# Halving the planner's slack between score pairs, and rearranging its two ends, in a fused attention and feed-forward kernel

## The chip, the cores and the metric

One core of a Trainium2 chip. The metric is the device time of one execution in microseconds (us). PE is TensorE, PEld its weight loads, DVE is VectorE, ACT is ScalarE, POOL is GpSimd, SP is SyncE; SPq and ACTq are the instruction queues that issue transfers. The time of a kernel is the median of its fast runs; ratios are the mean time of one kernel's fast runs over that of the other's fast runs of the same rounds, so they are not quite the ratio of the medians quoted. A profile covers one execution, and its span is some 1.7 us shorter than that run's time.

## The reference, cut to what matters

```python
x = A_x                                      # 2048 x 512, bf16
g = sigmoid((x * gate_w).sum(-1))            # one gate per row
qkv = x @ wqkv                               # 32 heads of width 16
p = softmax(q @ k.T / 4)                     # 2048 x 2048 for each head
a = (p @ v) @ wo
b = (silu(x @ w_gate) * (x @ w_up)) @ w_down # hidden width 1792
return g * a + (1 - g) * b
```

The exponentials of 32 x 2048 x 2048 scores are the bulk of the elementwise work.

## The kernel before

The program is written out by a planner in Python. A *unit* is the attention of four heads for 512 queries; there are 32, each of 64 *blocks* of 128 keys by 512 queries of one head. Two blocks form a *score pair*: TensorE writes it to one of two PSUM tiles `s_t`, ScalarE takes its exponential to `e_t`. Some blocks go to VectorE instead (`d_t`, then `y_t`), four to a *group*, with a chain of six further instructions. In what remains of the gap between two score pairs, TensorE does value products (`e_t` or `y_t` times `vaug`) and pieces of two matmuls of the projections and the feed-forward. The planner keeps an estimated clock for each engine, and lets a piece in if it overshoots the moment at which the next score tile comes free by at most `SLACK`:

```python
    def side(most):                          # the next projection or feed-forward piece, if it fits
        ...
        if t is None or t > plan.pe + 0.1 or 0.226 * mms + (0.1 if plan.mode != "F" else 0.0) > most:
            return None
        return c
...
    SLACK = 0.2
...
        room = s_end[pairs[0] % 2] - plan.pe
        if room > 0.02:
            if to_vector() and not d_wait and d_end[0] <= plan.pe + 0.05:
                vset.add(nxt)
                emit_d(nxt)                  # a block for VectorE has first call
                ...
            n_pv = pvs_ready(plan.pe)
            switch = 0.0 if plan.mode == "C" else 0.1
            fits = int((room + SLACK - switch) / 0.216)
            ...
            c = side(room + SLACK)
            if n_pv and fits > 0 and (...):
                emit_pv()                    # value products of one step
                ...
            if c is not None:
                pace.credit -= emit_piece(c)
                ...
        emit_pair(list(range(nxt, min(nxt + 2, nb))))
```

The start, up to the first score pair. The largest |k| of each head times |q| bounds the scores, and is subtracted ahead of the exponential:

```python
    act(out=q0r[:, :], in_=qp0[:, :], func=ACT.Copy)
    for i in range(2):
        vec.tensor_reduce(out=kpart0[:, i:i + 1], in_=kp0[i][:, :], axis=AX.X, op=ALU.max,
                          apply_absolute_value=True)
        vec.tensor_copy(out=ones_h[i][:], in_=onescol[:])
        act(out=kaug[:, 0, ...], in_=kp0[i][:, :], func=ACT.Identity, bias=ones_h[i][:, 0:1], scale=1.0)
        if i == 0:
            vec.tensor_scalar(out=aq0[:, :].bitcast(U16), in0=q0r[:, :].bitcast(U16), scalar1=0x7FFF,
                              scalar2=None, op0=ALU.bitwise_and)
        v0(8 * i)                            # values of the first heads: 32 small matmuls
    vec.tensor_scalar(out=kneg1, in0=bsel0, scalar1=kpart0[:, 0:1], ...)
    vec.scalar_tensor_tensor(out=kneg0, in0=bsel0, scalar=kpart0[:, 1:2], in1=kneg1, ...)
    mm(bp0[:, :], lhsT=kneg0, rhs=aq0[:, :], start=True, stop=True)
```

The end, after the last value product: `last_mm` works through the four row tiles in the order 2, 0, 1, 3.

```python
    for tq in range(TQ):
        vec.tensor_tensor(out=on_l[:, cs], in0=osb[:, cs], in1=rps[:, cs], op=ALU.mult)
    last_mm(1, on_l)
    act(out=scaled[:, :], in_=a_ps[2][:, 0:D], func=ACT.Identity, scale=gval[:, t:t + 1])
    nc.gpsimd.tensor_tensor(out=mt[:, 2, :], in0=scaled[:, :], in1=acc[0][:, 2, :], op=ALU.add)
    for tq in (0, 1, 3):
        store(qb * TQ + tq, a_ps[tq], acc[0][:, tq, :], mt[:, tq, :])    # VectorE, then a store from SyncE
    nc.sync.dma_start(out=out_f[t * P:(t + 1) * P, :], in_=mt[:, 2, :])
```

Of the kernel before, what the change touches and what calls it, by code (L numbers as in the profile page):

```python
# [8 lines left out]
ACT = mybir.ActivationFunctionType  # L9
ALU = mybir.AluOpType  # L10
# [3 lines left out]
U16 = mybir.dt.uint16  # L14
# [64 lines left out]
def kernel(  # L79
# [12 lines left out]
    nc = tc.nc  # L92
    P = 128
# [12 lines left out]
    TQ = QBW // P  # L106
    assert H * DH == D and D % P == 0 and F % P == 0 and S % QBW == 0 and G == 8 and TQ == 4
    out_f = out.flatten_outer_dims()
# [37 lines left out]
    def ordered(ins):  # L146
        i = ins.ins
        if i.engine in last_of:
            tc.add_manual_dep(
                i, last_of[i.engine].name,  # L150
                mybir.DependencyInfo(mybir.DependencyClass.NoSync, mybir.DependencyReason.DATA),
                reason="order",
            )
        last_of[i.engine] = i
        return ins
# [4 lines left out]
    def act(*args, **kw):  # L160
        ordered(nc.scalar.activation(*args, **kw))  # L161
# [7 lines left out]
    vec = Ordered()  # L169
# [6 lines left out]
    for c0 in (0, D):  # L176

        nc.scalar.dma_start(out=wqk[:, :, c0:c0 + 64],
                            in_=A_wqkv[:, c0:c0 + 64].rearrange("(dc p) c -> p dc c", p=P))
# [6 lines left out]
    for c0 in (D, 0):  # L186
        nc.sync.dma_start(out=wqk[:, :, c0 + 64:c0 + D],
                          in_=A_wqkv[:, c0 + 64:c0 + D].rearrange("(dc p) c -> p dc c", p=P))
# [18 lines left out]
    mt = big.tile([P, FC, QBW], BF16, name="mt")  # L207
# [3 lines left out]
    onescol = const.tile([P, 1], F32, name="onescol")  # L211
# [8 lines left out]
    bsel0 = mt[:, 3, 0:P]  # L220
# [3 lines left out]
    for i in range(2):  # L224
        nc.vector.tensor_copy(
            out=wpad[i][:, :, :].rearrange("p dc (j c) -> p dc j c", c=32)[:, :, :, 1:1 + DH],
            in_=wqk[:, :, i * D:i * D + 64].rearrange("p dc (j c) -> p dc j c", c=DH))
# [81 lines left out]
    def m_tile(name):  # L309
        while m_ready() is None:  # L310
            pay()
        plan.pe = max(plan.pe, m_ready())
        m_tiles[0] += 1
        return ps_m.tile([P, QBW], F32, tag="m", name=name)
# [63 lines left out]
    def v0(t0):  # L378

        p = m_tile("vp")  # L380
        for i in range(8):
            for dc in range(DC):
                mm(p[:, 64 * i:64 * i + 64], lhsT=xT[:, dc, (t0 + i) * P:(t0 + i + 1) * P], rhs=wv[:, dc, 0:64],
                   start=(dc == 0), stop=(dc == DC - 1))
        act(out=vaug[:, t0:t0 + 8, 0:4 * VC].rearrange("p t (h c) -> p t h c", c=VC)[:, :, :, 1:1 + DH],
            in_=p[:, :].rearrange("p (t h c) -> p t h c", h=4, c=DH), func=ACT.Copy)
        m_free(0.0)
# [433 lines left out]
    def store(t, a_ps, base, o_t=None):  # L821
        if o_t is None:
            o_t = opool.tile([P, D], BF16, tag="ot", name="o_t")[:, :]
        vec.scalar_tensor_tensor(out=o_t, in0=a_ps[:, 0:D], scalar=gval[:, t:t + 1], in1=base,
                                 op0=ALU.mult, op1=ALU.add)
        nc.sync.dma_start(out=out_f[t * P:(t + 1) * P, :], in_=o_t)
# [35 lines left out]
    qp0 = m_tile("qp0")  # L862
# [7 lines left out]
    kpart0 = const.tile([P, 2], F32, name="kpart0")  # L870
    ones_h = [const.tile([P, 1], F32, name=f"ones_h{i}") for i in range(2)]
    aq0 = work.tile([P, QBW], BF16, tag="aq", name="aq0", bufs=4)
    q0r = work.tile([P, QBW], BF16, tag="qst", name="q0r")
    kneg0 = mt[:, 3, P:2 * P]
    kneg1 = mt[:, 3, 2 * P:3 * P]
    act(out=q0r[:, :], in_=qp0[:, :], func=ACT.Copy)
    for i in range(2):
        vec.tensor_reduce(out=kpart0[:, i:i + 1], in_=kp0[i][:, :], axis=AX.X, op=ALU.max,
                          apply_absolute_value=True)
        vec.tensor_copy(out=ones_h[i][:], in_=onescol[:])  # L880
        act(out=kaug[:, 0, i * 2 * QBW:(i + 1) * 2 * QBW], in_=kp0[i][:, :], func=ACT.Identity,
            bias=ones_h[i][:, 0:1], scale=1.0)
        if i == 0:
            vec.tensor_scalar(out=aq0[:, :].bitcast(U16), in0=q0r[:, :].bitcast(U16), scalar1=0x7FFF, scalar2=None,
                              op0=ALU.bitwise_and)
        v0(8 * i)
    vec.tensor_scalar(out=kneg1, in0=bsel0, scalar1=kpart0[:, 0:1], scalar2=None, op0=ALU.mult)
    vec.scalar_tensor_tensor(out=kneg0, in0=bsel0, scalar=kpart0[:, 1:2], in1=kneg1,
                             op0=ALU.mult, op1=ALU.min)
    bp0 = ps_d.tile([P, QBW], F32, tag="d", name="bp0")  # L890
    mm(bp0[:, :], lhsT=kneg0, rhs=aq0[:, :], start=True, stop=True)
    for v in range(2):
# [1 line left out]
    for v in range(2):  # L894
        vec.scalar_tensor_tensor(out=q0[0][:, v, :], in0=bp0[:, :], scalar=vsel[:, v:v + 1],
                                 in1=q0[0][:, v, :], op0=ALU.mult, op1=ALU.add)
# [3 lines left out]
                            op0=ALU.is_gt, op1=ALU.mult)  # L900
    vec.scalar_tensor_tensor(out=bsel[:, :], in0=lo_t[:], scalar=0.5, in1=far_t[:],
                                   op0=ALU.is_lt, op1=ALU.mult)
# [50 lines left out]
    for qb in range(QB):  # L953
        a0 = f0 + per * qb
        for fc in range(FC):
            load, pcs = gu[(qb, fc)]
            i = order_.index((qb, fc))
# [117 lines left out]
    def side(most):  # L1075

        due = any(not c.out() for n in range(plan.slot, plan.slot + 12) for c in need.get(n, []))
        c = pace.next(plan.slot) if pace.credit > 0 or due else None
        if c is None:
            return None  # L1080
        mms, _, takes = c.pieces[c.i]
        t = m_ready() if takes else 0.0
# [3 lines that stand above are left out]
# [3 lines left out]
            pay_v() if vops else pay_d() if d_wait else pay()  # L1089
        emit_pv()  # L1090

    SLACK = 0.2
    def to_vector():

        un, at_ = divmod(nxt, 4 * KT)
        if vcur:
            if nxt % 4 in [b % 4 for b in vcur["b"]]:
                return 0
            return 2 if at_ >= 4 * KT - 4 * (NV - vcur["i"]) else 1
        if nxt < 16 or at_ > (50 if un < UNITS - 1 else 12) or y_live[0] >= 3 or sum(v[0] for v in vops) > 6:  # L1100
            return 0
        return 1

    while nxt < nb:
# [12 lines left out]
        if room > 0.02:  # L1117
# [6 lines left out]
            switch = 0.0 if plan.mode == "C" else 0.1  # L1124
            fits = int((room + SLACK - switch) / 0.216)
            crowded = pairs[0] - min(e_left.values(), default=pairs[0]) >= EB - 4
            c = side(room + SLACK)
            if n_pv and fits > 0 and (plan.mode == "C" or n_pv > 1 and fits > 1 and (pv_turn[0] or c is None)
# [59 lines left out]
               lhsT=rt[:, 4 * tq + j:4 * tq + j + 1].broadcast_to([P, 32]), rhs=ident[:, :],  # L1188
               start=True, stop=True, tile_position=(0, 32 * j), skip_group_check=True)
    on_l = work.tile([P, QBW], BF16, tag="rd", name="on_l")  # L1190
    for tq in range(TQ):
        cs = slice(tq * P, (tq + 1) * P)
        vec.tensor_tensor(out=on_l[:, cs], in0=osb[:, cs], in1=rps[:, cs], op=ALU.mult)
    last_mm(1, on_l)

    t = qb * TQ + 2
# [2 lines left out]
    nc.gpsimd.tensor_tensor(out=mt[:, 2, :], in0=scaled[:, :], in1=acc[0][:, 2, :], op=ALU.add)  # L1199
    for tq in (0, 1, 3):  # L1200
        store(qb * TQ + tq, a_ps[tq], acc[0][:, tq, :], mt[:, tq, :])
    nc.sync.dma_start(out=out_f[t * P:(t + 1) * P, :], in_=mt[:, 2, :])



# [28 lines left out]
```

## Time and profile before

| | before |
|---|---|
| time | 872.04 us (871.99 to 873.24) |
| span of the profile | 869.8 us |
| start, to the first exponential | 18.26 us |
| middle, first to last exponential | 840.74 us, 880 exponentials |
| end, from the start of the last exponential | 10.80 us |

The three parts sum to the span, and the edits fall into them one by one. These rows of the table by stretches have start and end, length, busy time and number of instructions of each engine, then the mean granted clock as a share of full speed, and DMA:

```profile
838.00:843.00 5.00, 3.43 (x32) 0.95 (x33) 4.90 (x11) 5.00 (x6) 0.00 (x0) 1.00 0.00 0
843.00:847.00 4.00, 4.00 (x22) 0.68 (x15) 2.24 (x5) 3.33 (x4) 0.00 (x0) 0.57 0.00 0
847.00:859.00 12.00, 9.70 (x69) 2.78 (x68) 6.33 (x8) 11.86 (x13) 0.00 (x0) 1.00 0.00 1
```

In the second row the clock is 0.57: 3.4 us of the 4 ran at half speed. ScalarE, busy all the time before, is busy 3.33 of 4.00 there.

### The profile page before, as it was taken

How to read it: one execution, taken by the hardware profiler on the slowest of the kernel's cores; microseconds unless marked ns; L12 is line 12 of the kernel's file. 1: busy time of each engine (PE TensorE's matmuls, PEld its weight loads, DVE VectorE, ACT ScalarE, POOL GpSimd, SP SyncE). 2: the span in 40 equal slices, each digit the busy share in tenths (PEclk: the TensorE clock that was granted, in tenths of full speed). 3: DMA queues.
4: the chain of work that ended last, by engine and by line, in shares of the span. 5: the costliest groups of instructions: out<-in, count | busy, mean ns of one | idle time of the engine just before them, and what ended most of it. 6: DMA issues, size and time to landing. Idle time of an engine off the chain costs nothing.

```text
span 869.8 us, 14419 instructions
## 1 busy us (share of the span) xinstructions
PE 798.7 (92%) x5232; PEld 208.8 (24%) x5232; DVE 796.5 (92%) x1117; ACT 842.7 (97%) x944; POOL 8.6 (1%) x31
## 2 busy tenths in 40 slices
PE   5999999999999999999999989989998989889985
PEld 2222222222222222222222222222222222222221
DVE  7889999999999999999999999989999999998974
ACT  3999999999999999999999999999999999999995
POOL 3000000000000000000000000000000000000000
PEclk9999999999999999999999999999999999999999
DMA  8400011111210012211000122110001121100000
GB/s 200 122 1 10 11 38 43 37 41 35 60 31 8 10 42 66 56 50 41 4 6 18 41 49 61 50 35 13 7 17 41 36 61 36 28 10 4 5 20 25
DMA packets 88064, 31.99 MB, mean 37 GB/s; under 512 B 75648, under 2 KB 87544, under 8 KB 87992
## 3 DMA queue, kind: packets, MB, share of 16 engines
q1 hardware_dynamic: 86408, 30.87, 14.5%
q8 instruction: 41, 0.67, 0.3%
q10 hardware_dynamic: 1584, 0.20, 0.1%
q14 instruction: 31, 0.25, 0.1%
HBM read 20.83 MB, written 2.34 MB: 27 GB/s over the span
## 4 chain that ended last, share of the span: by engine, by line
PE 46%; ACT 35%; DVE 8%; issue 8%; SPq 1%; DMA 1%; DVEq 0%; ACTq 0%
ACT e_t L161 33%; PE s_t L158 17%; PE o_ps L158 9%; PE dps L158 5%; PE d_t L158 4%; DVE y_t L167 4%; PE gp L158 3%; ACT th L161 3%; PE up L158 2%; DVE u_t L167 2%; PE a_ps L158 1%; PE qp L158 1%; PE vp L158 1%; PE kp L158 1%; PE x_ps L158 1%
## 5 line engine op out<-in xcount | busy, mean ns | idle before, releaser
L161 ACT ACTIVATE e_t<-s_t 128x1024 bf16<-128x1024 f32 x880 | 819.6, 1090 | 5.4 <-PE s_t L158 4.8
L158 PE MATMUL s_t<-qx,kaug 64*128 64x512 bf16 x1648 | 326.7, 384 | 47.7 <-ACT e_t L161 44.6
L167 DVE TENSOR_SCALAR y_t<-d_t 128x512 uint16<-128x512 f32 x288 | 197.8, 687 | 28.3 <-PE d_t L158 24.5
L158 PEld LDWEIGHTS <-kaug 64*128 64x128 bf16 x2048 | 99.6, 93 | 377.4 <-issue 374.3
L158 PE MATMUL o_ps<-e_t,vaug 128*32 128x512 bf16 x1760 | 172.0, 387 | 0.7 <-ACT e_t L161 0.7
L158 PE MATMUL d_t<-qx,kaug 64*128 64x512 bf16 x272 | 102.5, 377 | 0.6 <-DVE y_t L167 0.6
L167 DVE TENSOR_TENSOR y_t<-y_t,u_t 128x2048 uint16<-128x2048 uint16 x72 | 87.8, 1219 | 1.0
L167 DVE TENSOR_TENSOR u_t<-u_t 128x2048 f16<-128x2048 f16 x72 | 87.6, 1217 | 0.7
L167 DVE TENSOR_TENSOR u_t<-u_t,z_t 128x2048 f16<-128x2048 f16 x72 | 87.6, 1217 | 0.4
L158 PEld LDWEIGHTS <-vaug 128*32 128x32 bf16 x2048 | 45.1, 94 | 133.1 <-issue 130.2
L158 PE MATMUL dps<-wd_t,mt 128*128 128x512 bf16 x224 | 67.8, 384 | 0.0
L158 PE MATMUL gp<-xT,wg 128*128 128x512 bf16 x224 | 67.8, 384 | 0.0
L158 PE MATMUL up<-xT,wu 128*128 128x512 bf16 x224 | 64.7, 383 | 0.0
L167 DVE TENSOR_SCALAR y_t<-y_t 128x2048 uint16<-128x2048 uint16 x72 | 49.5, 688 | 1.2
L167 DVE TENSOR_SCALAR u_t<-z_t 128x2048 f16<-128x2048 uint16 x72 | 49.5, 687 | 0.8
L167 DVE TENSOR_SCALAR z_t<-y_t 128x2048 uint16<-128x2048 uint16 x72 | 49.3, 684 | 0.2
L167 DVE SCALAR_TENSOR_TENSOR mt<-gs,up 128x512 bf16<-128x512 bf16 x56 | 38.2, 682 | 4.7 <-PE up L158 3.4
L167 DVE SCALAR_TENSOR_TENSOR gs<-th,gp 128x512 bf16<-128x512 bf16 x56 | 38.2, 682 | 2.6 <-ACT th L161 2.3
L161 ACT ACTIVATE th<-gp 128x512 bf16<-128x512 f32 x56 | 36.7, 655 | 0.0
L158 PEld LDWEIGHTS <-mt 128*128 128x128 bf16 x263 | 16.2, 99 | 43.2 <-issue 35.1
L158 PE MATMUL s_t<-on,kaug 64*128 64x512 bf16 x112 | 22.4, 383 | 1.8 <-ACT e_t L161 1.4
L158 PEld LDWEIGHTS <-wu 128*128 128x128 bf16 x224 | 14.2, 97 | 30.1 <-issue 24.7
(104 smaller groups left out, 358.0 us busy)
## 6 DMA issues: line engine op xcount, KB each, us to landing
wg<-in_B_w_gate_dram SPq DMA_DIRECT2D x56, 128.0 KB
wu<-in_B_w_up_dram SPq DMA_DIRECT2D x56, 128.0 KB
on<-osb SPq DMA_DIRECT2D x120, 16.0 KB
rb<-rr SPq DMA_DIRECT2D x15, 128.0 KB
wd_t<-in_B_w_down_dram SPq DMA_DIRECT2D x1, 1792.0 KB
qx<-qst SPq DMA_DIRECT2D x112, 16.0 KB
out_dram<-o_t SPq DMA_DIRECT2D x12, 128.0 KB
kaug<-on SPq DMA_DIRECT2D x20, 64.0 KB
```

The costliest lines, as they stand in the source:

```text
L158: ordered(nc.tensor.matmul(*args, **kw))
L161: ordered(nc.scalar.activation(*args, **kw))
L167: return lambda *a, **kw: ordered(f(*a, **kw))
```

## The change

Its intent: less overshoot in each gap, so that ScalarE finds its scores ready; 0.29 us and one product less on VectorE's chain at the start; and stores that don't queue behind one another at the end. The diff, cut to its core:

```diff
     act(out=q0r[:, :], in_=qp0[:, :], func=ACT.Copy)
+    act(out=aq0[:, :], in_=qp0[:, :], func=ACT.Abs)
     for i in range(2):
         vec.tensor_reduce(out=kpart0[:, i:i + 1], ...)
-        vec.tensor_copy(out=ones_h[i][:], in_=onescol[:])
+        if i == 0:
+            vec.tensor_copy(out=ones_h[0][:], in_=onescol[:])
+            vec.tensor_scalar(out=kneg1, in0=bsel0, scalar1=kpart0[:, 0:1], ...)
+        else:
+            vec.scalar_tensor_tensor(out=kneg0, in0=bsel0, scalar=kpart0[:, 1:2], in1=kneg1, ...)
+            vec.tensor_copy(out=ones_h[1][:], in_=onescol[:])
         act(out=kaug[:, 0, ...], ...)
-        if i == 0:
-            vec.tensor_scalar(out=aq0..., scalar1=0x7FFF, op0=ALU.bitwise_and)
         v0(8 * i)
-    vec.tensor_scalar(out=kneg1, ...)
-    vec.scalar_tensor_tensor(out=kneg0, ...)
...
-    SLACK = 0.2
+    SLACK = 0.1
...
-    for tq in range(TQ):
+    for tq in (2, 0, 1, 3):
         vec.tensor_tensor(out=on_l[:, cs], ...)
...
-    nc.sync.dma_start(out=out_f[t * P:(t + 1) * P, :], in_=mt[:, 2, :])
+    nc.scalar.dma_start(out=out_f[t * P:(t + 1) * P, :], in_=mt[:, 2, :])
```

More of the change, by code (lines that the diff above doesn't have):

```diff
@@ L879 @@
                           apply_absolute_value=True)
-        vec.tensor_copy(out=ones_h[i][:], in_=onescol[:])
+        if i == 0:
+            vec.tensor_copy(out=ones_h[0][:], in_=onescol[:])
+            vec.tensor_scalar(out=kneg1, in0=bsel0, scalar1=kpart0[:, 0:1], scalar2=None, op0=ALU.mult)
+        else:
+            vec.scalar_tensor_tensor(out=kneg0, in0=bsel0, scalar=kpart0[:, 1:2], in1=kneg1,
+                                     op0=ALU.mult, op1=ALU.min)
+            vec.tensor_copy(out=ones_h[1][:], in_=onescol[:])
         act(out=kaug[:, 0, i * 2 * QBW:(i + 1) * 2 * QBW], in_=kp0[i][:, :], func=ACT.Identity,
             bias=ones_h[i][:, 0:1], scale=1.0)
-        if i == 0:
-            vec.tensor_scalar(out=aq0[:, :].bitcast(U16), in0=q0r[:, :].bitcast(U16), scalar1=0x7FFF, scalar2=None,
-                              op0=ALU.bitwise_and)
         v0(8 * i)
-    vec.tensor_scalar(out=kneg1, in0=bsel0, scalar1=kpart0[:, 0:1], scalar2=None, op0=ALU.mult)
-    vec.scalar_tensor_tensor(out=kneg0, in0=bsel0, scalar=kpart0[:, 1:2], in1=kneg1,
-                             op0=ALU.mult, op1=ALU.min)
     bp0 = ps_d.tile([P, QBW], F32, tag="d", name="bp0")
```

## The prediction

> **What bounds the kernel now.** I read the page's busy shares first, then its groups, then the waits of ScalarE, then ScalarE's timeline, and last the timelines of the two ends, where three of the four edits lie.
>
> ```profile
> PE 798.7 (92%) x5232; PEld 208.8 (24%) x5232; DVE 796.5 (92%) x1117; ACT 842.7 (97%) x944; POOL 8.6 (1%) x31
> ...
> L161 ACT ACTIVATE e_t<-s_t 128x1024 bf16<-128x1024 f32 x880 | 819.6, 1090 | 5.4 <-PE s_t L158 4.8
> L158 PE MATMUL s_t<-qx,kaug 64*128 64x512 bf16 x1648 | 326.7, 384 | 47.7 <-ACT e_t L161 44.6
> L167 DVE TENSOR_SCALAR y_t<-d_t 128x512 uint16<-128x512 f32 x288 | 197.8, 687 | 28.3 <-PE d_t L158 24.5
> ```
>
> ScalarE is busy 97%, nearly all of it in 880 exponentials of score pairs; TensorE waits 44.6 us for it. So ScalarE carries the middle. But 5.4 us of idle time understates what can be won: the mean record is 1090 ns, longer than the distance from one exponential to the next, because records overlap. The floor is in the start times:
>
> ```profile
> 399.67 6.58 ACT L161 ACTIVATE e_t<-s_t 128x1024 bf16<-128x1024 f32 x7
> 405.99 0.75 ACT L161 ACTIVATE th<-gp 128x512 bf16<-128x512 f32 x1
> 406.47 5.78 ACT L161 ACTIVATE e_t<-s_t 128x1024 bf16<-128x1024 f32 x6
> 412.68 8.36 ACT L161 ACTIVATE e_t<-s_t 128x1024 bf16<-128x1024 f32 x9 [0.44 <-PE s_t L158]
> ```
>
> Seven exponentials from 399.67 to the tanh at 405.99 are (405.99 - 399.67) / 7 = 0.903 us each; the tanh takes 406.47 - 405.99 = 0.48. The first exponential starts at 18.26, the last at 859.00, as ScalarE's timeline and the chain show: 840.7 us. The floor is 879 x 0.903 + 56 x 0.48 = 820.6. So **20 us in the middle are bubbles**, most too small to be listed as idle. That is all that better spacing can give while the exponentials stay 880.
>
> What makes a bubble, in the timeline of all engines near 202:
>
> ```profile
> 201.67 0.39 PE L158 MATMUL s_t<-qx,kaug 64*128 64x512 bf16 x2
> ...
> 202.00 0.60 PE L158 MATMUL kp<-xT,wqk 128*128 128x512 bf16 x2
> ...
> 202.53 0.40 PE L158 MATMUL o_ps<-e_t,vaug 128*32 128x512 bf16 x3
> ...
> 202.86 0.39 PE L158 MATMUL s_t<-qx,kaug 64*128 64x512 bf16 x2
> ```
>
> Between two score pairs TensorE ran a projection piece and a value product; the next pair then started 1.19 us after the one before, where the floor is 0.90. In the chain of waits the exponentials of this place start at 202.23 and 203.35, 1.12 apart: a bubble of 0.21.
>
> **What the Trainium skill says.** "ScalarE: Activation LUTs", section "Table sets: the hidden batching unit", says that abs is in every table set as filler, so the new Abs should need no further table load. The trace shows the cost of one (1.28 us, once, at 2.37 us) and, agreeing, that Copy, Identity, Exp and Tanh share it. The section "What ACT_TABLE_LOAD costs" says back-to-back activations overlap by about 93 ns; here 1085 (median) - 903 = 182 ns, and I use the trace. "DMA: Bandwidth & Descriptors", section "Issuing engines are not separate DMA queues", says that several issuing engines only save the issue time of the sequencer. The tail below shows that this issue time, and an in-order wait, are what the last stores pay.
>
> **Part 1, queries' magnitudes and first bound.** The start now:
>
> ```profile
> 14.51 0.29 DVE L167 TENSOR_SCALAR aq<-q0r 128x512 uint16<-128x512 uint16 x1
> ...
> 14.72 1.22 DVE L167 TENSOR_REDUCE kpart<-kp 128x1 f32<-128x1024 f32 x1
> ...
> 16.19 0.35 DVE L167 SCALAR_TENSOR_TENSOR mt<-mt,kpart 128x128 bf16<-128x128 bf16 x1
> 16.46 0.61 DVE L167 TENSOR_SCALAR qx<-q0r,vsel 128x512 bf16<-128x512 bf16 x2
> ...
> 17.03 1.41 DVE L167 SCALAR_TENSOR_TENSOR qx<-bp,vsel,qx 128x512 bf16<-128x512 f32 x2
> ```
>
> VectorE is the chain here. The mask of 0.29 us leaves it and the first product of the bound (0.24) takes that place, so the second maximum starts at about the same 14.7. After it, instead of copy, product, combination (15.93 to 16.55 in the chain), only the combination remains: some 0.35 us earlier. Against this, ScalarE gets an Abs of a 512-wide tile out of PSUM, start to start about 0.48 like the tanh. It pushes the two copies of keys back by about 0.3, and since the projection's PSUM tile is freed only after it, the second block of first-head values waits to about 15.0 instead of 14.7. TensorE had 0.89 us idle before the bound's matmul, so this is hidden. I put **-0.35 us** on the first exponential (18.26 to about 17.9).
>
> **Part 2, the tail.**
>
> ```profile
> 862.39 0.88 DVE L167 TENSOR_TENSOR on_l<-osb,rps 128x128 bf16<-128x128 bf16 x4 [0.52 <-PE rps L158]
> 863.13 0.54 PEld L158 LDWEIGHTS <-on_l 128*128 128x128 bf16 x4 [0.97 <-DVE on_l L167]
> ...
> 864.33 1.26 POOL L1199 TENSOR_TENSOR mt<-scaled,kaug 128x512 bf16<-128x512 f32 x1 [856.03 <-ACT scaled L161]
> 865.32 0.74 DVE L167 SCALAR_TENSOR_TENSOR mt<-a_l,gval,kaug 128x512 bf16<-128x512 f32 x1
> 865.62 0.36 SPq L1202 DMA_DIRECT2D out_dram<-mt  x1
> 866.08 1.37 SPq L826 DMA_DIRECT2D out_dram<-mt  x3
> ```
>
> TensorE takes tile 2 first, but VectorE makes it third. Making it first takes two steps of 0.22 off: -0.44 on the path over ScalarE, GpSimd and VectorE. The larger thing is the queue: the store of tile 2 stands first in it and waits for GpSimd (864.33 + 1.26 = 865.59), and the other three follow at 0.46 each, the last at about 867.0, though two of their tiles were ready by 865.4. On ScalarE's queue tile 2 goes at about 865.2 by itself, and the last of the three is issued when its data are ready: 866.06 - 0.44 + 0.1 = 865.7. So the last issue moves by 867.0 - 865.7 = **-1.3 us**, the first part included. The transfers fill the engines for about 0.5 us each, so they don't collide.
>
> **Part 3, the slack, and where I chose.** The program plans each gap and lets a piece of TensorE work in when it ends at most SLACK after the next score tile comes free. I went through the planner's decisions for the kernel before beside the trace, and classed all 880 gaps by the planned overshoot and the bubble measured after them: up to 0.1 us, 602 gaps carry 4.8 us; 0.1 to 0.15, 137 gaps 2.9 us; 0.15 to 0.2, 121 gaps 9.7 us; beyond, 20 gaps 2.0 us. By content, 58 gaps of one projection piece and one value product carry 6.5 us, and 53 of a VectorE score and two value products 2.3 us. These are what a slack of 0.1 refuses, so **at most about 12 us** are in reach.
>
> But the refused work is not dropped. 98 projection pieces and 137 value products were let in by the slack alone. They need other gaps, and only 79 gaps are empty and 39 hold a VectorE score alone. TensorE's 45 us of waiting for ScalarE is a bare cover for about 98 x 0.55 + 137 x 0.25 = 88 us of work, some of which replaces what also moves. So part of it will meet full gaps, run late, or be forced by a deadline. I let under half of the reach come through: **-4.3 us**. This halving is a choice, not a measurement.
>
> Sum: 872.0 - 0.35 - 1.3 - 4.3 = **866.0 us**.
>
> **The rivals.** (a) TensorE becomes the bound: the deferred pieces pile up and run after the last exponential, or in forced bursts. For it: 92% busy, and the supply of empty gaps above. Against: it still waits for ScalarE in 112 places, up to 1 us. Ten pieces left over would cost 10 x 0.55 = 5.5 us and eat the gain: about 870 to 872. (b) The division of labour shifts: 72 groups of four blocks go to VectorE now. Value products that come later hold their buffers, and each group lost gives ScalarE two more exponentials, 1.8 us; three lost is 5.4 us, again about 871. For it: three such buffers only; against: scores for VectorE have first call on a gap. (c) The tail is hidden by something else: if the end is set by transfers already running, the 1.3 us shrink; the queue rows speak against it. (d) The reach comes through whole, because ScalarE's cushion takes the moved pieces: 872 - 1.65 - 10 = about 860. The clock was 0.97 of full between 800 and 860; bubbles of 0.3 to 0.6 us near 844 to 847 go with it, and could go or double: 1 us either way.
>
> **Range and chances.** Ends alone give 870.4; the middle between +1 and -10 gives 871.5 to 860.5, which I take as the range. Faster by over 2% means below 854.6, 17 of the 20 us of bubbles: 0.02. Slower by over 2% means above 889.5, ten groups lost or 17 us of forced bursts: 0.02. Within 2%: 0.96.
>
> **What would show it.** Right: still 880 exponentials and 288 VectorE scores; far fewer gaps with a projection piece and a value product; first to last exponential about 836 instead of 840.7; the first exponential near 17.9; one table load; from the start of the last exponential to the end 9.5 us instead of 10.8 (869.8 - 859.0), with stores from two queues. Wrong: more than 880 exponentials; projection pieces after the last exponential; long idle stretches of ScalarE in place of many short ones; a second table load before the first exponential.

## The result, and the profile after

The changed kernel takes **866.72 us** (866.48 to 868.7, four runs) beside 872.01 us; ratio 0.9941, 95% interval 0.9924 to 0.9958: 0.6% faster, which is clear of noise but within the 2% that counts as the same.

| | before | after | difference | predicted |
|---|---|---|---|---|
| start | 18.26 | 18.22 | -0.04 | -0.35 |
| middle | 840.74 | 837.13 | -3.61 | -4.3 |
| end | 10.80 | 9.45 | -1.35 | -1.3 |
| span | 869.8 | 864.8 | -5.0 | -6.0 |

The page's groups after, which answer to the first fence of the prediction (busy us, mean ns; then idle time and what ended it):

```profile
L161 ACT ACTIVATE e_t<-s_t 128x1024 bf16<-128x1024 f32 x880 | 822.5, 1137 | 1.9 <-PE s_t L158 0.8
L158 PE MATMUL s_t<-qx,kaug 64*128 64x512 bf16 x1648 | 331.1, 382 | 44.3 <-ACT e_t L161 39.5
L167 DVE TENSOR_SCALAR y_t<-d_t 128x512 uint16<-128x512 f32 x288 | 198.0, 688 | 30.8 <-PE d_t L158 27.1
```

The counts of 880 and 288 are the same: no work changed engines in the middle. ScalarE's listed idle time before exponentials fell from 5.4 to 1.9 us, and TensorE's wait for ScalarE from 44.6 to 39.5. Busy time can't tell more: the mean record even grew, to 1137 ns, at the same distance of 0.904 us.

The start after, from the timeline (start, length, engine, instruction):

```profile
13.46 1.23 DVE L167 TENSOR_REDUCE kpart<-kp 128x1 f32<-128x1024 f32 x1 [1.80 <-PE kp L158]
...
14.60 0.59 ACT L161 ACTIVATE aq<-qp 128x512 bf16<-128x512 f32 x1
...
14.89 1.22 DVE L167 TENSOR_REDUCE kpart<-kp 128x1 f32<-128x1024 f32 x1
...
15.24 1.09 PE L158 MATMUL vp<-rb,xT 128*128 128x64 bf16 x32 [0.24 <-ACT aq L161]
...
16.14 0.35 DVE L167 SCALAR_TENSOR_TENSOR mt<-mt,kpart 128x128 bf16<-128x128 bf16 x1
...
17.00 1.40 DVE L167 SCALAR_TENSOR_TENSOR qx<-bp,vsel,qx 128x512 bf16<-128x512 f32 x2
```

The input landed later in this execution: the first maximum starts at 13.46, before at 13.23. From the first maximum to the first exponential it is 18.22 - 13.46 = 4.76 us, before 18.26 - 13.23 = 5.03. So 0.27 of the 0.35 us came, and a late transfer hid them. The value matmuls wait for the Abs, as foreseen; they end at 15.24 + 1.09 = 16.33, ahead of the combination's end at 16.49, so that wait costs nothing.

The end after:

```profile
858.75 0.88 DVE L167 TENSOR_TENSOR on_l<-osb,rps 128x128 bf16<-128x128 bf16 x4 [0.51 <-PE rps L158]
859.09 0.39 PE L158 MATMUL a_l<-wo_l,on_l 128*128 128x512 bf16 x1 [0.40 <-DVE on_l L167]
...
860.73 1.65 SPq L826 DMA_DIRECT2D out_dram<-mt  x3
861.28 0.74 DVE L167 SCALAR_TENSOR_TENSOR mt<-a_l,gval,kaug 128x512 bf16<-128x512 f32 x1
861.59 0.37 ACTq L1203 DMA_DIRECT2D out_dram<-mt  x1
```

TensorE starts 0.34 us after the first product instead of 0.74, and SyncE's stores begin when their own data are ready, not after GpSimd's tile. The last of them is issued at 860.73 + 1.65 = 862.38, 3.63 us after the products began; before it was 867.45 - 862.39 = 5.06.

### The profile page after: what moved, and what is told of

Read it like the earlier page. It is cut to its first block, busy times and chain, and to the rows that moved or that the text cites. A ratio compares the mean times of both kernels' runs of the same rounds, so it can differ in the third digit from the quotient of the medians.

```text
span 864.8 us, 14339 instructions
## 1 busy us (share of the span) xinstructions
PE 787.3 (91%) x5145; PEld 217.4 (25%) x5232; DVE 797.0 (92%) x1119; ACT 842.4 (97%) x945; POOL 8.7 (1%) x31
## 4 chain that ended last, share of the span: by engine, by line
PE 41%; ACT 39%; DVE 9%; issue 9%; SPq 1%; DMA 1%; DVEq 0%; ACTq 0%
ACT e_t L161 36%; PE s_t L158 15%; PE o_ps L158 7%; PE d_t L158 4%; DVE y_t L167 4%; PE dps L158 4%; ACT th L161 3%; PE gp L158 3%; DVE u_t L167 2%; PE up L158 2%; PE kp L158 1%; PE vp L158 1%; DVE mt L167 1%; PE qp L158 1%; PE x_ps L158 1%
## 5 line engine op out<-in xcount | busy, mean ns | idle before, releaser
L161 ACT ACTIVATE e_t<-s_t 128x1024 bf16<-128x1024 f32 x880 | 822.5, 1137 | 1.9 <-PE s_t L158 0.8
L158 PE MATMUL s_t<-qx,kaug 64*128 64x512 bf16 x1648 | 331.1, 382 | 44.3 <-ACT e_t L161 39.5
L158 PEld LDWEIGHTS <-kaug 64*128 64x128 bf16 x2048 | 109.7, 93 | 380.9 <-issue 376.8
L158 PE MATMUL o_ps<-e_t,vaug 128*32 128x512 bf16 x1760 | 169.9, 386 | 0.5 <-ACT e_t L161 0.5
L158 PE MATMUL dps<-wd_t,mt 128*128 128x512 bf16 x205 | 63.5, 384 | 2.5 <-issue 2.5
L158 PE MATMUL gp<-xT,wg 128*128 128x512 bf16 x202 | 62.9, 384 | 2.4 <-issue 2.4
L158 PE MATMUL up<-xT,wu 128*128 128x512 bf16 x205 | 60.9, 383 | 2.1 <-issue 2.1
L161 ACT ACTIVATE th<-gp 128x512 bf16<-128x512 f32 x56 | 40.3, 720 | 0.0
L167 DVE TENSOR_TENSOR osb<-of,x_ps 128x512 bf16<-128x512 f32 x30 | 20.4, 680 | 1.2 <-PE x_ps L158 1.2
```

Of the source, the lines that this page charges most:

```text
L158: ordered(nc.tensor.matmul(*args, **kw))
L161: ordered(nc.scalar.activation(*args, **kw))
L167: return lambda *a, **kw: ordered(f(*a, **kw))
```

## The experiments

All twelve gave correct results. For reading the middle I use one measure: the distance from each exponential's start to the next, less 0.904 us, and less 0.476 for a tanh in between, is that gap's *bubble*. The gaps are classed by what the program puts into them in order, as recorded while it was built: F a projection or feed-forward piece, P a step of value products, d a block for VectorE. Thus FP is a piece followed by value products.

### One part of the change at a time

For the slack alone, the diff is `SLACK = 0.2` to `0.1`, and nothing else.

> The kernel before with SLACK 0.1 alone. If the parts add, the first-to-last exponential distance is 837.1 us as in the changed kernel (840.7 before) and the time falls by 3.6 us, to about 868.4. Rival: the parts interact (an earlier start or another end shifts the buffers), then it differs from -3.6 by more than 1 us. Both: 880 exponentials and 288 VectorE scores.

Measured: 869.68 us beside 873.01, ratio 0.9964 (0.9950 to 0.9979). The middle is 836.71 us. It is 4.0 us shorter than before's, within half a microsecond of the changed kernel's: no interaction of the parts shows.

The end alone: only the two hunks at the end of the diff.

> The kernel before with the two tail edits alone (order of the last four products, last store of tile 2 from ScalarE's queue). Theory: from the start of the last exponential to the end 9.45 us instead of 10.8, so -1.35 us, about 870.7. Rival: the end is set by transfers, and the gain belongs to the middle: then under -0.5.

Measured: 871.56 us, ratio 0.9985 (0.9974 to 0.9997). The end is 9.40 us instead of 10.80, so -1.40, as the theory says.

The start alone: only the hunk at its top.

> The kernel before with the start edits alone. Theory: from the first maximum to the first exponential 4.76 us instead of 5.03, so -0.27 us, which the time hardly resolves (871.8); to be read from the profile. Rival: Abs on ScalarE holds the chain, then no shorter than 5.03.

Measured: 872.06 us, ratio 0.9994 (0.9980 to 1.0007), not told from nothing by the time. In the profile, first maximum to first exponential is 4.76 us, just as in the changed kernel.

The product of the three ratios is 0.9964 x 0.9985 x 0.9994 = 0.9943, beside 0.9941 for the whole. The gain is accounted for, some three fifths of it by the slack; the interval of each factor is about 0.0013 to either side.

### Which half of the slack

`SLACK` stands in two places. The first experiment limits value products only:

```diff
-            fits = int((room + SLACK - switch) / 0.216)
+            fits = int((room + 0.1 - switch) / 0.216)
```

> The kernel before with 0.1 of slack for value products only; projection pieces keep 0.2. The gaps with a projection piece followed by a value product fall from 58 to 5 in the program (7 with SLACK 0.1 everywhere). Theory: these gaps made the bubbles, so most of the middle's gain is here: -2.5 to -4.5 us. Rival: the gain came from holding back projection pieces; then within 1 us of before.

Measured: 869.81 us, ratio 0.9971 (0.9958 to 0.9985), at the lower edge of the expected gain. By the times it can't be told from slack_only. The profile's middle, 838.62 us, is 2.1 us shorter than before's where slack_only's is 4.0 shorter, so that most of the gain is here is not shown. The second limits pieces only:

```diff
-            c = side(room + SLACK)
+            c = side(room + 0.1)
```

> The kernel before with 0.1 of slack for projection pieces only; value products keep 0.2. In the program, gaps with a projection piece followed by a value product rise from 58 to 102, and gaps with a VectorE score followed by a projection piece fall from 56 to 46. Theory: the first kind makes the bubbles (6.5 us / 58 = 0.11 us each), so the middle gets 44 x 0.11 = 4.9 us longer at most, and the time lies 2 to 5 us above before. Rival: holding projection pieces back is the good half of the edit: then 1 to 3 us below before.

Measured: 880.04 us beside 872.78, ratio 1.0076 (1.0063 to 1.0088). The sign is the theory's, the size is above its 2 to 5 us: the middle is 846.33, 5.6 us longer. ScalarE's list of waits in this kernel (total us, times, longest):

```profile
ACT e_t L161 <- PE s_t L158: 9.4, 14, 1.3
```

Before it was 4.8 us with the longest 0.7. And the end grew to 13.36 us, because eleven matmuls of the output projection and more were still to do after the last exponential. The pieces that the narrow limit refused were caught up late.

Nor is the middle's loss the theory's. The FP gaps, as the table below shows, carry only 1.3 us more; gaps of two pieces in a row (FF) carry 5.1 us more, 5.5 of their 6.0 in four gaps, near 22, 249, 327 and 511 us. The first lies at the end of a half-clock stretch. In the other three a late piece of the next heads' bound follows its query projection at once, and between them TensorE waits 1.11 us for VectorE's magnitudes of those queries (`aq`); the lists of TensorE's waits in the kernel before and in the changed one have no such wait:

```profile
247.73 0.38 PE L158 MATMUL bp<-aq,kneg 128*8 128x512 bf16 x1 [1.11 <-DVE aq L167]
...
248.53 1.94 ACT L161 ACTIVATE e_t<-s_t 128x1024 bf16<-128x1024 f32 x2 [1.33 <-PE s_t L158]
```

So the sign came out right, but mostly by another cause than the theory's.

A third experiment refuses only value products that would follow a piece:

```diff
-            fits = int((room + SLACK - switch) / 0.216)
+            fits = int((room + (0.1 if plan.mode == 'F' else SLACK) - switch) / 0.216)
```

> The kernel before with 0.1 of slack only for a value product that would follow a projection piece. Those gaps fall from 58 to none in the program, and nothing else is refused. Theory: first-to-last exponential shorter by 6.5 us less what comes back elsewhere (2.9 us in the changed kernel), so -3 to -5 us outside half-clock stretches. Rival: the bubbles only move to the gaps that take the refused value products (49 with a VectorE score and two products, 25 with three products): then within 1 us of before, and those two classes rise by over 2 us.

Measured: 871.69 us beside 872.78, ratio 0.9980 (0.9967 to 0.9993). The middle is 837.79 us, but with 878 exponentials, worth 2 x 0.904 = 1.8 us; at equal work it is 1.1 us shorter than before (each of the two profiles has one half-clock stretch in its middle). The end is 12.14 us, with a group of VectorE's finished only after the last exponential (more of that below). My theory that this class alone carries the gain fell, and the rival is nearer. The classes show it (gaps, then us of bubbles):

| kernel | FP | dPP | PPP | dF | Fd | PP | FF | all |
|---|---|---|---|---|---|---|---|---|
| before | 58, 6.5 | 53, 2.3 | 18, 1.7 | 56, 0.7 | 23, 0.4 | 106, 0.6 | 26, 0.9 | 19.4 |
| changed | 7, 0.0 | 41, 2.9 | 24, 1.5 | 50, 1.5 | 40, 1.6 | 115, 1.5 | 23, 1.1 | 15.8 |
| slack_only | 7, 0.0 | 41, 2.9 | 24, 1.9 | 50, 1.7 | 40, 1.5 | 115, 1.4 | 23, 0.9 | 15.3 |
| fits_only | 5, 0.0 | 39, 2.2 | 16, 1.7 | 66, 2.2 | 36, 1.0 | 132, 0.9 | 19, 0.9 | 17.2 |
| after_projection_only | 3, 0.0 | 49, 2.6 | 25, 3.4 | 74, 1.8 | 15, 0.4 | 106, 0.4 | 23, 1.0 | 18.2 |
| side_only | 102, 7.8 | 35, 1.8 | 21, 0.7 | 46, 0.1 | 40, 0.7 | 104, 0.5 | 27, 6.0 | 25.0 |

The 6.5 us of the FP gaps vanish wherever those gaps are refused, and 7.8 stand at 102 of them. But much of this is paid out again in the gaps that take the refused work: of 6.5 us, 2.9 in the changed kernel and 5.3 with only this one refusal, where they are PPP, dF and dP (0.4 us before, 1.4 here). In these profiles neither limit gives the whole effect alone, and one of them alone is a loss.

### The value of the slack

Two neighbours of the changed kernel, with `SLACK = 0.12` and `SLACK = 0.05`.

> The changed kernel with 0.12 of slack for projection pieces and value products. Gaps with a projection piece and a value product: 4 in the program. Theory (the gain comes from a whole class of gaps refused, not from the fine value): within 1 us of the changed kernel, 866 to 867.7 beside before at 872 to 873. Rival (the schedule is chaotic and 0.1 was a lucky draw): 2 us or more above it.

> The changed kernel with 0.05 of slack. In the program 34 projection pieces are left over after the last exponential (468 fit in the loop instead of 502), and only 44 gaps are empty. Theory (TensorE's free gaps run out): projection pieces run after the last exponential and the end part grows by several us, time at or above the kernel before. Rival (less slack is simply better): below 866.

Measured at 0.12: 870.39 us beside 872.78, ratio 0.9970 (0.9958 to 0.9983), some 3.7 us above the changed kernel's 866.72 (2.5 us by the ratios, as the two ran in different rounds): the rival's size. Yet the bubbles are not the cause: they sum to 16.1 us beside 15.8, and the middle is 835.65 with 878 exponentials. It is the end that grew, from 9.45 to 14.50 us. The last exponential starts at 854.0; the timeline then:

```profile
856.38 1.21 DVE L167 TENSOR_TENSOR y_t<-y_t,u_t 128x2048 uint16<-128x2048 uint16 x1
857.63 0.69 DVE L167 TENSOR_SCALAR y_t<-y_t 128x2048 uint16<-128x2048 uint16 x1
858.38 0.62 PE L158 MATMUL x_ps<-y_t,vaug 128*32 128x512 bf16 x4 [2.64 <-DVE y_t L167]
```

A 73rd group for VectorE is being finished after ScalarE is done, and TensorE waits 2.64 us for it. The group is not all of the 5 us: in this profile the granted clock is 0.50 from 854.0 to the span's end. From the first of the last four products (861.92) to that end it is 6.58 us, where the changed kernel has 6.05, and no group is left to wait for there.

Measured at 0.05: 891.91 us, ratio 1.0214 (1.0200 to 1.0228), slower by over 2%. TensorE's gaps have run out, as the theory says, but the size, 19 us, surprised me. My count of 34 pieces left over was wrong in one point: 15 of them are forced inside the loop, and 19 come after the last exponential. There are 878 exponentials here too, so a 73rd group. The profiled run is the slowest of the five, 895.16 us. The timeline around 196 us:

```profile
195.46 0.23 DVE L167 TENSOR_SCALAR kneg<-bsel,kb 128x8 bf16<-128x8 bf16 x1
195.74 0.59 PE L158 MATMUL bp<-aq,kneg 128*8 128x512 bf16 x1 [3.37 <-DVE kneg L167]
...
196.97 1.02 ACT L161 ACTIVATE e_t<-s_t 128x1024 bf16<-128x1024 f32 x1 [6.25 <-PE s_t L158]
```

and the stretches around it:

```profile
184.00:195.00 11.00, 6.27 (x40) 1.90 (x39) 9.43 (x13) 6.72 (x8) 0.00 (x0) 1.00 0.10 24
195.00:206.00 11.00, 9.93 (x39) 1.59 (x39) 4.80 (x10) 6.83 (x8) 0.00 (x0) 0.53 0.35 66
206.00:217.00 11.00, 10.65 (x69) 2.96 (x70) 10.80 (x16) 10.92 (x14) 0.00 (x0) 1.00 0.16 37
```

Key projections that were put off come due at once. The next heads' bound needs them, TensorE waits 3.37 us for VectorE's maximum, and ScalarE idles 6.25 us. In the second stretch the mean clock is 0.53, and ScalarE is busy only 6.83 of 11 us, the last 2 us of that idle time included. Three more such half-clock stretches lie near 103, 342 and 714 us. Ahead of the last two TensorE waited 1.48 and 2.35 us for the transfer of a late bound (`qx<-bq`), ahead of the first no longer than 0.6. The end is 16.88 us, with put-off pieces of the feed-forward and the output projection.

To test the reading of 0.12, the last experiment of this kind forbids the late group:

```diff
-        if nxt < 16 or at_ > (50 if un < UNITS - 1 else 12) or y_live[0] >= 3 or ...:
+        if nxt < 16 or at_ > (50 if un < UNITS - 1 else 4) or y_live[0] >= 3 or ...:
```

with `SLACK = 0.12`.

> The kernel with SLACK 0.12, but in the last unit no new group of four blocks may go to VectorE after the fifth block (limit 4 instead of 12). With SLACK 0.12 the program had 73 such groups and 878 exponentials, the middle was 835.65 us, and the end 14.50 us instead of 9.45. Theory (the 73rd group, formed in the last unit, is finished by VectorE after the last exponential, and that is what the end pays): 880 exponentials, 288 VectorE scores, middle 837.5, end 9.45, time near 866. Rival (projection pieces pushed late make the end longer): the end stays above 12 us.

Measured: 868.54 us beside 872.45, ratio 0.9959 (0.9945 to 0.9973). There are 880 exponentials again and the end is 9.41 us, so the late group was the cause of the long end. The half clock from the last exponential on went with it; whether the group brings it about was not tested. The middle is 838.66, 1.2 us above what I expected: bubbles of 17.3 us, 2.3 of them in PP gaps. This does not beat the changed kernel, and no version that I ran does. The rival of a lucky draw is not refuted: a step of 0.02 moved one whole group, and what is left of the difference (ratio 0.9959 beside 0.9941) lies within the two intervals.

### The parts of the two ends

First the order alone, then the queue alone.

> The kernel before with the order of the last four products alone (tile 2 first). Theory: tile 2's store, first in its queue, is released 0.44 us earlier and the other three follow it, so from the start of the last exponential to the end 10.36 us instead of 10.80. Rival: without the second queue the order gives nothing, 10.8.

```profile
858.00:862.00 4.00, 3.69 (x18) 1.10 (x17) 0.69 (x1) 1.78 (x2) 0.00 (x0) 0.57 0.02 4
...
865.72 0.36 SPq L1202 DMA_DIRECT2D out_dram<-mt  x1
866.18 1.38 SPq L826 DMA_DIRECT2D out_dram<-mt  x3
```

The end is 11.20 us, longer than before's, and the first line says why: a half-clock stretch (0.57) fell on it. So I count from the first of the four products, 862.88 here, to the span's end, 869.9, behind that stretch: 7.02 us, before 869.8 - 862.39 = 7.41. That is -0.39, near the -0.44 expected. Tile 2's store is still first in the one queue, only earlier.

> The kernel before with tile 2's store on ScalarE's queue alone. Theory: the other three stores no longer wait for GpSimd; the last is issued when its tile is ready, near 866.15 instead of 867.0: 9.9 to 9.95 us instead of 10.80. Rival: the transfers themselves set the end: above 10.5.

```profile
867.05 1.65 SPq L826 DMA_DIRECT2D out_dram<-mt  x3
867.60 0.74 DVE L167 SCALAR_TENSOR_TENSOR mt<-a_l,gval,kaug 128x512 bf16<-128x512 f32 x1
867.90 0.37 ACTq L1202 DMA_DIRECT2D out_dram<-mt  x1
```

The end is 9.82 us, -0.98. With the products' start at 864.67 and a span of 871.1 the count from there is 6.43, also -0.98, a little more than the -0.85 to -0.9 expected. The two add to -1.37; the changed kernel's count is 864.8 - 858.75 = 6.05, so -1.36. Transfers did not set the end.

For the start, the mask goes back to VectorE while the bound's first product stays early:

```diff
-    act(out=aq0[:, :], in_=qp0[:, :], func=ACT.Abs)
...
             vec.tensor_scalar(out=kneg1, in0=bsel0, scalar1=kpart0[:, 0:1], ...)
+            vec.tensor_scalar(out=aq0[:, :].bitcast(U16), in0=q0r[:, :].bitcast(U16), scalar1=0x7FFF, ...)
```

> The changed kernel with the magnitudes' mask put back on VectorE ahead of the second maximum, the bound's products left where the change put them. Theory (only work taken off VectorE's chain counts): from the first maximum to the first exponential 4.95 to 5.05 us instead of 4.76, so nearly the whole gain of the start is the move to ScalarE. Rival (the reordering of the bound is what helps): 4.8 or less.

```profile
14.60 1.22 DVE L167 TENSOR_REDUCE kpart<-kp 128x1 f32<-128x1024 f32 x1 [2.25 <-PE kp L158]
...
16.22 0.29 DVE L167 TENSOR_SCALAR aq<-q0r 128x512 uint16<-128x512 uint16 x1
16.43 1.22 DVE L167 TENSOR_REDUCE kpart<-kp 128x1 f32<-128x1024 f32 x1
```

First maximum to first exponential is 5.16 us, no shorter than before's 5.03: the second maximum starts 16.43 - 14.60 = 1.83 us after the first, where the changed kernel has 14.89 - 13.46 = 1.43. The move to ScalarE is what counts. What exceeds the range is a wait of VectorE's: in this execution ScalarE's copy, which the mask reads, came 0.99 us after the first maximum instead of 0.65. By estimate the mask lost 0.1 to 0.2 us so, and reordering alone would give 0.05 us, not more.

## Why the prediction was right

The time of 866.72 us lies 0.7 us from the 866.0 predicted. By its steps:

**The bound.** That ScalarE's chain of exponentials carries the middle, with some 20 us of bubbles, held: its floor stayed 0.904 us, and what moved was bubbles.

**The start.** Right in kind: the Abs needed no table load and its hold on the value matmuls was hidden. The -0.35 us was -0.27. I took 0.35 for the copy and the product ahead of the combination. It starts 16.14 - 14.89 = 1.25 us after the second maximum does, before 16.19 - 14.72 = 1.47, so they were worth 0.22; small shifts before and after it make up the rest.

**The end.** -1.3 predicted, -1.35 measured. The split between order and queue, -0.44 and the rest, was -0.39 and -0.98 in single profiles.

**The slack.** -4.3 predicted, -3.6 in the profile. The mechanism held for FP gaps, 58 with 6.5 us down to 7 with none. Two terms were mis-sized. First, the reach. By the prediction's own classes the gaps that overshoot by more than 0.1 us carried 2.9 + 9.7 + 2.0 = 14.6 us, not about 12, and I counted the dPP gaps as refused; 41 of 53 stayed, and cost more than before, 2.9 us. Second, what comes back in other gaps was larger. I sorted the gaps by planned overshoot again, each kernel's planner beside its trace: those above 0.1 us fall from 278 with 14.5 us of bubbles to 65 with 3.4, but those below rise from 601 with 4.9 to 814 with 12.5. So 11.1 us went and 7.6 came back, in gaps that the rule allows; a small planned overshoot does not by itself keep a gap free of a bubble.

The profile before contains a half-clock stretch in its middle (the 0.57 above, with bubbles of some 1.3 us), and the one after none. The old schedule in a profile without such a stretch in the middle (order_only) has a middle of 839.57; the new one has 836.71 to 837.13 in three profiles (the changed kernel, slack_only, mask_on_vector). The other profiles of the old schedule, tail_only, start_only and queue_only (841.79 to 842.44), have one or two such stretches each in the middle; without the bubbles beside them all five lie at 838.9 to 840.5. So the spacing itself gives about 2.4 to 2.9 us by these single profiles (an estimate), under a quarter of the 12 us in reach, where I allowed a little over a third. The sum came out nearer than this term did, as the half-clock stretch went the same way; that part is luck. In the range, "17 of the 20 us" for faster by over 2% leaves out what the ends give: 870.35 - 854.6 = 15.75 of bubbles would do.

**The rivals.** (a), TensorE running out of gaps, does not show in the changed kernel but lies right beside it: at 0.05 it costs 19 us, over three times what I gave it, with ScalarE stalled by put-off pieces, and three of four half-clock stretches in or just behind such stalls; in side_only it begins. (b), another division of labour, also did not occur at 0.1, but at 0.12, at 0.05 and in after_projection_only it did, in the other direction: a group too many, at 0.12 with 5 us at the end. (c) is refuted by queue_only, and (d) by the classes.

What stays open is whether the new spacing makes half-clock stretches rarer. Four of the five profiles of the old schedule have one in the middle, none of the three of the new. 11 timed runs of the kernel before had a mean clock of 0.994 to 0.998, the changed kernel 0.998, 0.999, 0.999 and 0.994, and slack_only 0.994 to 0.999. The slack_only runs follow their clock: 867.74 us at 0.999, 869.17 at 0.996, 870.19 to 871.03 at 0.994. No experiment set the clock apart.

## What to carry to other kernels

Where one engine's instructions overlap in the records, take the distance of their starts as the floor, and sum what exceeds it by the content of the gap: idle time listed 5.4 us here, and 19.4 were there. Work that a tighter rule refuses is not gone; count the gaps that must take it, and expect most of the gain to be paid back, or all of it when they run out. And a queue that issues in order should not have the store with the slowest producer first.

## What the Trainium skill lacked or had wrong

- "ScalarE: Activation LUTs", section "What ACT_TABLE_LOAD costs": back-to-back activations overlap by about 93 ns there. Here the median exponential of 1024 columns took 1085 ns and the next began 0.904 us after it, an overlap of 181 ns. Nor is the record's length fixed: its mean went from 1090 to 1137 ns with the change, at the same distance.
- "DMA: Bandwidth & Descriptors", section "Issuing engines are not separate DMA queues": it says that a second issuing engine saves only issue time, usually small beside the transfer. Here a second queue saved 0.98 us of the end: issue takes 0.46 us for each store, and a store whose data are late holds back those issued behind it. The section does not mention the second.
- "TensorE: Matmul & The Clock Gate", section "HAM oscillation — how this bites in real kernels": the rule there is to have no idle gap above about 3.4 us. The half-clock stretch of the kernel before lasted 3.4 us, as the page's window has it, but in the 5 us ahead of it TensorE was busy 3.43 us and no wait exceeded 0.6 us. The page's next section speaks of short idle gaps that do the same; no threshold is given.
- No page that I know of says what half-clock stretches in the middle of a kernel do to comparisons: within one kernel (slack_only) runs spread from 867.74 to 871.03 us with the mean clock from 0.999 to 0.994, as much as the whole effect of the slack. That the clock causes the spread is not shown.
